# Linear attention into a rational feed-forward layer on one core: the weight conversions go by single chunks, GpSimd's signs move one slot ahead, and the first Newton step stands behind the first pair of chunks

## The chip, the core and the metric

The kernel runs on one core of one Trainium2 chip. The time is what the device takes for one launch, in microseconds (us). Before the change it is 920.56 us, the median of three runs (919.81 to 922.37). One execution was also recorded by the hardware profiler; it took 918.86 us, and its span, from the first to the last instruction, is 917.1 us. Engines are called as in the profile: PE (TensorE's matmuls) with PEld (its weight loads), DVE (VectorE), ACT (ScalarE), POOL (GpSimd), SP (the queue that issues most transfers).

## The reference, cut to what matters

```python
kv  = einsum('bhsd,bhse->bhde', k, v)          # 8 batches, 8 heads, 576 tokens, 64 wide
out = einsum('bhsd,bhde->bhse', q, kv)
rms = sqrt(mean(out * out, axis=-1) + 1e-06)
x   = (out / rms * g_norm)                     # laid out as 4608 tokens x 512
h   = x @ w_in                                 # 512 x 2048
P   = a[0] + a[1]*h + a[2]*h**2 + a[3]*h**3
Q   = 1 + |b[0]|*|h| + |b[1]|*h**2
y   = (P / (Q + 1e-06)) @ w_out                # 2048 x 512
```

`w_in` and `w_out` are float64, all else is float32. The two weight matrices go to the chip as their raw 64-bit words, and the kernel itself makes float32 numbers of them.

## The kernel before, in words

**Tiles and slots.** The 4608 tokens are nine tiles of 512, and the hidden width of 2048 is sixteen chunks of 128. The program walks over 144 *slots* (tile t, chunk c), numbered i = 16 t + c. In a slot, TensorE's first product makes h for the slot that follows (`gemm1`: `h_c`, 128 hidden channels by 512 tokens). ScalarE and VectorE make the rational function of it (`ew_a`, `ew_b`, `ew_c`: d, q and u, the result being g), and TensorE's second product adds the chunk that was finished two slots before to four accumulators (`gemm2`, `acc`). In tile 0 both products take plain float32 operands: a matmul of 128x512 is two instructions, so `h` and `acc` take eight each. From tile 1 on each operand is split into a coarse and a fine part of a faster type, and a product takes three matmuls (lines 445 to 447 and 506 to 508). The attention of tile t+1 runs inside the slots of tile t: `kvp` in slots 1, 3, 5 and 7 of tile 0, `op` in 2, 4, 6 and 8, the mean squares and the Newton step of the norm in slot 9, the norms in 12 and 13, the splitting of x and of the first weights in 14.

**What sets the order.** Each engine takes its instructions in the order in which the program writes them. That order is written out by hand, in slots, and by the table `schedule`, which gives each pair of chunks (a *unit*: `("wi", 4)` is chunks 4 and 5 of `w_in`, `("wo", 2)` chunks 2 and 3 of `w_out`) three slot numbers: when it is fetched, when ScalarE scales it, and when it is split for tile 1. Waits between engines follow from who reads what the other writes.

**Conversion.** A unit lies in memory as `raw`, 128 partitions of 1024 64-bit words, each a low and a high 32-bit word. A chunk is half of it, 512 words. The float32 number is made in four steps: `conv_a` scales the high words (an f32 product, in place) and turns the low words into what has to be added (in place); the sign is brought into the result tile; the high word, shifted left by three bits, is put beside the sign; and the low part is added. For units from `u2` on, `conv_a` is done by ScalarE (line 190, two instructions over 1024 words). The sign is made by GpSimd (`signs`, line 214: high word times 0.0), and VectorE does the other two steps (`conv_c`: line 218, shift and OR; line 222, the addition, a custom instruction). `conv_b` is another form in which VectorE makes the sign itself, with three instructions (lines 208 to 210). The first two units are converted ahead of the slots, with `conv_a` on VectorE (line 188).

**Where conversions stand before.** The list `made` says how many chunks VectorE converts at the end of slot k, in the order in which units are fetched: one in slots 0 and 1, two in 2 and 3, three in 4, two in 5, three in 6, and two in each of 7 to 13. `parts_at` joins two chunks of one unit into one instruction over 1024 words. GpSimd's signs of a chunk are issued in the same slot as its conversion, held back behind that slot's q (line 457), so that they run while VectorE reads h from PSUM. The conversion is the last thing of the slot on VectorE, behind the attention's small subtraction (`kvl`, line 277) and behind the Newton step (lines 287 and 288) in slot 9.

**Ahead of the slots.** VectorE converts chunk 0 with `conv_b` (signs by itself), chunk 1 and chunk 2 with GpSimd's signs, and between chunk 2's two last steps it runs the Newton step of the first tile's norm. Then TensorE spreads the norm over partitions (`rb`, line 620), VectorE multiplies x by it four times (line 621), and chunk 3 is converted. The first product (`h_0`) takes x as it comes.

Of the kernel before, what the change touches and what calls it, by code (L numbers as in the profile page):

```python
# [9 lines left out]
I32 = mybir.dt.int32  # L10
# [13 lines left out]
def linear_attention_then_rational_ffn(  # L24
# [93 lines left out]
    def f32(t):  # L118
        return t.bitcast(F32)
# [27 lines left out]
    def at_slot(step, k):  # L147
        return [u for u in units if schedule[u][step] == k]

    chunks = [(u, j) for u in units for j in range(2)][4:]
    made = {}
    for k, n in enumerate([1, 1, 2, 2, 3, 2, 3] + 7 * [2]):
        made[k], chunks = chunks[:n], chunks[n:]
    assert not chunks

    def unsplit(t, c):
        return t == 0 or t == 1 and c >= LATE
# [31 lines left out]

    def conv_a(u, part=both, engine="S"):
        low, high = words(u, part)
        scale(engine, f32(high), f32(high), 2.0**-112)
        scale(engine, low, low.bitcast(U32), 2.0**-29)

    def room(u):
        kind, c = u
# [3 lines left out]
                w32[kind, c + j] = ups[u][:, j * DM:(j + 1) * DM]  # L202
        return ups[u]

    def conv_b(u, part=both):
        low, high = words(u, part)
        w = room(u).bitcast(I32)[:, part]
        DVE.tensor_scalar(w, high, 3, None, ALU.logical_shift_left)
        DVE.scalar_tensor_tensor(w, high, -(1 << 31), w, ALU.bitwise_and, ALU.bitwise_or)
        DVE.tensor_tensor(w, w, low, ALU.add)  # L210

# [1 line left out]
    def signs(u, part):  # L213
        return POOL.tensor_scalar(room(u)[:, part], f32(words(u, part)[1]), 0.0, None, ALU.mult)

    def conv_c1(u, part):
        w = ups[u].bitcast(I32)[:, part]
        DVE.scalar_tensor_tensor(w, words(u, part)[1], 3, w, ALU.logical_shift_left, ALU.bitwise_or)  # L218

    def conv_c2(u, part):  # L220
        w = ups[u].bitcast(I32)[:, part]
        DVE.tensor_tensor(w, w, words(u, part)[0], ALU.add)

    def conv_c(u, part):
        conv_c1(u, part)
        conv_c2(u, part)

    def parts_at(k):
        out = []
        for u, j in made.get(k, []):  # L230
            if out and out[-1][0] == u:
                out[-1] = u, both
            else:
                out.append((u, (one, two)[j]))
        return out

    def gpart(k, j):
        if k not in gparts:
# [358 lines left out]
        PE.matmul(ms0[p * Q4:(p + 1) * Q4], sel, sq0[p], start=True, stop=True)  # L597
    warm(14, ps_acc.tile([P, TW], F32, tag="acc", name="idle2"))
    u0, u1, u2 = units[:3]
    for u, part in ((u0, two), (u1, one), (u1, two)):  # L600
        signs(u, part)
    conv_a(u0, one, "V")
    conv_b(u0, one)
    conv_a(u0, two, "V")
    conv_c(u0, two)
    conv_a(u1, one, "V")
    conv_c1(u1, one)
    r0 = work.tile([P, TW], F32, tag="u", name="r_0")
    r2 = work.tile([P, TW], F32, tag="u", name="r2_0")
    newton_rstd(ms0, r0, r2)()  # L610
    conv_c2(u1, one)
    ACT.copy(x0[:, NPAIR - 1], o0[NPAIR - 1])
    ACT.activation(b1abs, abg[:, 5:6], AF.Abs)
    conv_a(u2)
    signs(u2, both)
    for p in range(NPAIR):
        pool, tag, bufs = ((ps_h, "h", 2), (ps_h, "h", 2), (ps_at, "at", 1), (ps_at, "ms", 1))[p]
        rb = pool.tile([P, TW], F32, tag=tag, name=f"rb_0_{p}", bufs=bufs)
        ps = slice(p * Q4, (p + 1) * Q4)
        PE.matmul(rb, spread[ps], r0[ps], start=True, stop=True)  # L620
        DVE.scalar_tensor_tensor(x0[:, p], x0[:, p], ghalf, rb, ALU.mult, ALU.mult)
    conv_a(u1, two, "V")
    conv_c(u1, two)


    slots = [(t, c) for t in range(NTILE) for c in range(NF)]
# [1 line left out]
    ph = gemm1(0, 0)  # L628
    for i, (t, c) in enumerate(slots[:-1]):
        q_made = ew_a(t, c, ph)  # L630
        for k, (u, part) in enumerate(parts_at(i) if i > 1 else []):
            made_signs = signs(u, part)
            if k == 0:

                tc.add_manual_dep(made_signs.ins, q_made.ins.name, beside, reason="signs beside h")
        if i:
            ew_d(*slots[i - 1])
        rest = {0: [], 1: [], 2: []}
        ew_b(t, c, ph)
        for u in at_slot(2, i):  # L640
            rest[2].append(split_w(u))
        for u in at_slot(1, i):
            conv_a(u)
        if i >= LAG:
            gemm2(*slots[i - LAG])
            if slots[i - LAG][1] == NF - 1:
                evacuate(slots[i - LAG][0])
        if i < 4:
            ph = gemm1(0, i + 1)
        if t + 1 < NTILE:  # L650
            for step, p in (attention0 if t == 0 else attention)[c]:
# [59 lines left out]
```

## Time and profile before

| what | value |
|---|---|
| median of three runs | 920.56 us |
| profiled execution, its own time | 918.86 us |
| its span | 917.1 us |
| PE busy | 898.5 us (98%) |
| DVE busy | 797.0 us (87%) |
| ACT busy | 685.2 us (75%) |
| POOL busy | 52.7 us (6%), all of it in the first sixth |
| mean granted TensorE clock | 0.996 |

The share of PE is a union of the matmuls' modelled spans, so a PE that is busy may still have been given its work late; the waits and the stretches of the trace tell that. Tile 0, which takes the first sixth of the span, is the only place in which weights are converted, and it is the stretch that the change touches. In a row of the timeline the two first numbers are the start and the time in us, counted from the span's start; what stands in brackets is the idle time of the engine before it and what ended it.

### The profile page before, as it was taken

To read this page: it belongs to the slowest core of one execution; us is meant where nothing else is said; L and a number is where in the kernel's file an instruction comes from. 1 tells how busy PE (TensorE), PEld (TensorE's weight loads), DVE (VectorE), ACT (ScalarE), POOL (GpSimd) and SP (SyncE) were. 2 spreads that over 40 slices of the span, in tenths; PEclk is the share of its full clock that TensorE was granted. 3 is DMA by queue.
4 is the path that set the end of the run, shared out by engine and by line. 5 is a ranking of instruction groups with operands and counts; after the bars stand their busy time and mean duration, and the time that the engine had idled before them with its cause. 6 is when DMAs were issued, how large, how long until landed. Compare 5 with 4: busy or idle time off the path is not lost.

```text
span 917.1 us, 11675 instructions
## 1 busy us (share of the span) xinstructions
PE 898.5 (98%) x4284; PEld 677.8 (74%) x4284; DVE 797.0 (87%) x1237; ACT 685.2 (75%) x1163; POOL 52.7 (6%) x60
## 2 busy tenths in 40 slices
PE   7979998999999999999999999999999999999998
PEld 5434444777768788878887888788887888788886
DVE  3888899999988899889987997889878988898887
ACT  4667776988677768777876787777867787777665
POOL 5134340000000000000000000000000000000000
PEclk9999999999999999999999999999999999999999
DMA  9846100221032012211231213110311020101001
GB/s 368 320 164 232 35 25 30 97 81 47 2 117 72 20 46 89 78 41 48 75 93 41 48 41 117 50 48 21 107 52 48 0 69 13 48 0 46 1 1 46
DMA packets 23961, 65.89 MB, mean 72 GB/s; under 512 B 2336, under 2 KB 2336, under 8 KB 23904
## 3 DMA queue, kind: packets, MB, share of 16 engines
q1 hardware_dynamic: 23328, 64.10, 21.5%
q10 hardware_dynamic: 576, 1.05, 0.3%
q8 instruction: 33, 0.54, 0.2%
q14 instruction: 24, 0.20, 0.1%
HBM read 55.58 MB, written 9.57 MB: 71 GB/s over the span
## 4 chain that ended last, share of the span: by engine, by line
PE 79%; DVE 11%; ACT 6%; issue 2%; DMA 2%; POOL 0%; ACTq 0%; DVEq 0%
PE h L445 12%; PE h L447 12%; PE h L446 12%; PE acc L506 11%; PE acc L507 11%; PE acc L508 11%; PE acc L502 2%; PE kvp L329 2%; DVE q L457 2%; ACT d L466 1%; PE h L441 1%; ACT d L467 1%; DVE u L473 1%; DMA raw_wi<-in_w_in_dram 1%; DVE wow L218 1%
## 5 line engine op out<-in xcount | busy, mean ns | idle before, releaser
L445 PE MATMUL h<-x,parts 128*128 128x512 f32 (+1 forms) x516 | 205.4, 398 | 0.0
L455 ACT ACTIVATE d<-h 128x512 f32<-128x512 f32 x143 | 85.7, 599 | 159.8 <-PE h L447 147.0
L447 PE MATMUL h<-x,parts 128*128 128x512 f32 (+1 forms) x516 | 200.5, 389 | 0.0
L507 PE MATMUL acc<-wol,gh 128*128 128x512 f32 x492 | 191.6, 389 | 0.7 <-DVE wol L259 0.7
L457 DVE SCALAR_TENSOR_TENSOR q<-d,b1abs,q 128x512 f32<-128x512 f32 x143 | 107.1, 749 | 84.5 <-ACT q L456 84.4
L446 PE MATMUL h<-x,wil 128*128 128x512 f32 (+1 forms) x452 | 175.5, 388 | 0.0
L506 PE MATMUL acc<-parts,gl 128*128 128x512 f32 x440 | 171.6, 390 | 0.2 <-DVE gl L490 0.2
L508 PE MATMUL acc<-parts,gh 128*128 128x512 f32 x440 | 171.2, 389 | 0.0
L466 ACT ACTIVATE d<-q,bias 128x512 f32<-128x512 f32 x143 | 105.3, 736 | 36.6 <-DVE q L457 35.7
L445 PEld LDWEIGHTS h<-x,parts 128*128 128x128 f32 x516 | 96.9, 188 | 26.8 <-DVE gl L490 5.0
L447 PEld LDWEIGHTS h<-x,parts 128*128 128x128 f32 x516 | 96.9, 188 | 20.6
L458 ACT ACTIVATE u<-h,na 128x512 f32<-128x512 f32 x143 | 112.0, 783 | 0.0
L473 DVE SCALAR_TENSOR_TENSOR u<-u,na,d 128x512 f32<-128x512 f32 x143 | 107.9, 754 | 0.0
L507 PEld LDWEIGHTS acc<-wol,gh 128*128 128x128 f32 x492 | 92.3, 188 | 20.1 <-DVE wol L259 1.0
L467 ACT ACTIVATE d<-d,bias 128x512 f32<-128x512 f32 x143 | 103.6, 724 | 4.7
L465 DVE SCALAR_TENSOR_TENSOR u<-u,na,h 128x512 f32<-128x512 f32 x143 | 106.2, 743 | 0.7
L471 DVE SCALAR_TENSOR_TENSOR q<-q,d 128x512 f32<-128x512 f32 x143 | 98.5, 689 | 2.9 <-ACT d L467 2.7
L459 DVE TENSOR_TENSOR u<-u,h 128x512 f32<-128x512 f32 x143 | 97.9, 685 | 0.9
L456 ACT ACTIVATE q<-h,abg 128x512 f32<-128x512 f32 x143 | 97.9, 685 | 0.0
L446 PEld LDWEIGHTS h<-x,wil 128*128 128x128 f32 x452 | 85.0, 188 | 16.2 <-issue 0.2
L506 PEld LDWEIGHTS acc<-parts,gl 128*128 128x128 f32 x440 | 82.6, 188 | 18.5 <-DVE gl L490 1.1
L508 PEld LDWEIGHTS acc<-parts,gh 128*128 128x128 f32 x440 | 82.6, 188 | 17.2
(142 smaller groups left out, 1124.4 us busy)
## 6 DMA issues: line engine op xcount, KB each, us to landing
kvm<-in_kv_dram SPq DMA_DIRECT2D x28, 640.0 KB
raw_wo<-in_w_out_dram SPq DMA_DIRECT2D x8, 1024.0 KB
qr<-in_qT_dram SPq DMA_DIRECT2D x32, 256.0 KB
out_dram<-ob SPq DMA_DIRECT2D x16, 512.0 KB
rb<-rd SPq DMA_DIRECT2D x28, 256.0 KB
raw_wi<-in_w_in_dram SPq DMA_DIRECT2D x6, 1024.0 KB
first<-in_first_dram SPq DMA_DIRECT2D x4, 640.0 KB
raw_wi<-in_w_in_dram SPq DMA_DIRECT2D x4, 512.0 KB
```

The costliest lines, as they stand in the source:

```text
L445: PE.matmul(ph, wh, xl, start=(kc == 0), stop=False)
L446: PE.matmul(ph, wl, xh, start=False, stop=False)
L447: PE.matmul(ph, wh, xh, start=False, stop=(kc == NPAIR - 1))
L457: q_made = DVE.scalar_tensor_tensor(q, d, b1abs, q, ALU.mult, ALU.add)
L458: ACT.activation(u, ph, AF.Identity, bias=na[:, 2:3], scale=na[:, 3:4])
L465: DVE.scalar_tensor_tensor(u, u, na[:, 1:2], ph, ALU.add, ALU.mult)
L466: ACT.activation(d, q, AF.Ln, bias=bias[:, 2:3], scale=QSC)
L467: ACT.activation(d, d, AF.Exp, bias=bias[:, 3:4], scale=-1.0)
L473: DVE.scalar_tensor_tensor(u, u, na[:, 0:1], d, ALU.add, ALU.mult)
L506: PE.matmul(o, gl[:, ss], wh, start=(c == 0), stop=False)
L507: PE.matmul(o, gh[:, ss], wl, start=False, stop=False)
L508: PE.matmul(o, gh[:, ss], wh, start=False, stop=(c == NF - 1))
```

## The change

It does five things. (1) Chunks are converted one at a time, in the order in which the products of tile 0 take them: w_out's chunk c, then w_in's chunk c+3, two in each of slots 0 to 13 and the last in slot 15; no two chunks are joined. (2) The first chunk of a slot stands ahead of the attention's work and of the Newton step on VectorE, the second behind. (3) GpSimd's signs are made by whole units, in the slot in which ScalarE scales the unit, which is a slot or more ahead of the conversion. GpSimd therefore reads the high words before ScalarE overwrites them; so ScalarE scales the low words first. (4) Ahead of the slots the signs of chunks 1, 2 and 3 are made by VectorE (`conv_b1` and `conv_b2`, three instructions a chunk), not by GpSimd. (5) The Newton step stands behind the first two chunks; chunk 2's conversion is begun ahead of the four norm products and ended behind them, and chunk 3's is begun before slot 0 and ended in it. PE, ACT and SP keep their order, but for the swap of ScalarE's two scalings.

```diff
-    chunks = [(u, j) for u in units for j in range(2)][4:]
-    made = {}
-    for k, n in enumerate([1, 1, 2, 2, 3, 2, 3] + 7 * [2]):
-        made[k], chunks = chunks[:n], chunks[n:]
-    assert not chunks
+    order = []
+    for c in range(NF):
+        order += [(("wo", c - c % 2), c % 2)]
+        order += [(("wi", c + 3 - (c + 3) % 2), (c + 3) % 2)] if c + 3 < NF else []
+    made = {k: order[2 * k:2 * k + 2] for k in range(NF - 2)}
+    made[NF - 1] = order[2 * (NF - 2):]
...
     def conv_a(u, part=both, engine="S"):
         low, high = words(u, part)
+        scale(engine, low, low.bitcast(U32), 2.0**-29)
         scale(engine, f32(high), f32(high), 2.0**-112)
-        scale(engine, low, low.bitcast(U32), 2.0**-29)
...
-    def conv_b(u, part=both):
+    def conv_b1(u, part):
+        DVE.tensor_scalar(room(u).bitcast(I32)[:, part], words(u, part)[1], 3, None, ALU.logical_shift_left)
+
+    def conv_b2(u, part):
         low, high = words(u, part)
-        w = room(u).bitcast(I32)[:, part]
-        DVE.tensor_scalar(w, high, 3, None, ALU.logical_shift_left)
+        w = ups[u].bitcast(I32)[:, part]
         DVE.scalar_tensor_tensor(w, high, -(1 << 31), w, ALU.bitwise_and, ALU.bitwise_or)
         DVE.tensor_tensor(w, w, low, ALU.add)
...
-    for u, part in ((u0, two), (u1, one), (u1, two)):
-        signs(u, part)
-    conv_a(u0, one, "V")
-    conv_b(u0, one)
-    conv_a(u0, two, "V")
-    conv_c(u0, two)
-    conv_a(u1, one, "V")
-    conv_c1(u1, one)
+    for part in (one, two):
+        conv_a(u0, part, "V")
+        conv_b1(u0, part)
+        conv_b2(u0, part)
     r0 = work.tile([P, TW], F32, tag="u", name="r_0")
     r2 = work.tile([P, TW], F32, tag="u", name="r2_0")
     newton_rstd(ms0, r0, r2)()
-    conv_c2(u1, one)
+    conv_a(u1, one, "V")
+    conv_b1(u1, one)
...
+    signs(u2, both)
     conv_a(u2)
-    signs(u2, both)
     for p in range(NPAIR):
...
         DVE.scalar_tensor_tensor(x0[:, p], x0[:, p], ghalf, rb, ALU.mult, ALU.mult)
+    conv_b2(u1, one)
     conv_a(u1, two, "V")
-    conv_c(u1, two)
+    conv_b1(u1, two)
...
         q_made = ew_a(t, c, ph)
-        for k, (u, part) in enumerate(parts_at(i) if i > 1 else []):
-            made_signs = signs(u, part)
-            if k == 0:
-
-                tc.add_manual_dep(made_signs.ins, q_made.ins.name, beside, reason="signs beside h")
+        for u in at_slot(1, i):
+
+            tc.add_manual_dep(signs(u, both).ins, q_made.ins.name, beside, reason="signs beside h")
...
             conv_a(u)
+        convs = [lambda u=u, j=j: (conv_b2 if u == u1 else conv_c)(u, (one, two)[j]) for u, j in made.get(i, [])]
+        rest[2] += convs[:1]
...
-        for u, part in parts_at(i):
-            rest[2].append(lambda u=u, part=part: conv_c(u, part))
+        rest[2] += convs[1:]
```

VectorE ahead of the slots. `raw_wi_149` is the unit of chunks 0 and 1, `raw_wi_152` that of chunks 2 and 3; `ms` and `r` are the Newton step, `x` the four norm products. Before:

```order
L188 TENSOR_SCALAR raw_wi_149<-raw_wi_149 128x512 x2
L218 SCALAR_TENSOR_TENSOR wiw_280<-raw_wi_149,wiw_280 128x512
L222 ISA wiw_280<-raw_wi_149,wiw_280 128x1024
L188 TENSOR_SCALAR raw_wi_152<-raw_wi_152 128x512 x2
L218 SCALAR_TENSOR_TENSOR wiw_282<-raw_wi_152,wiw_282 128x512
L287 SCALAR_TENSOR_TENSOR r_0_298<-ms_260,r_0_298 128x512
L288 SCALAR_TENSOR_TENSOR r_297<-r_0_298,r_297 128x512
L222 ISA wiw_282<-raw_wi_152,wiw_282 128x1024
L621 SCALAR_TENSOR_TENSOR x_157<-x_157,ghalf,rb_0_311 128x512
```

The same place with the change:

```order
L189 TENSOR_SCALAR raw_wi_149<-raw_wi_149 128x512 x2
L207 TENSOR_SCALAR wiw_282<-raw_wi_149 128x512
L212 SCALAR_TENSOR_TENSOR wiw_282<-raw_wi_149,wiw_282 128x512
L213 ISA wiw_282<-raw_wi_149,wiw_282 128x1024
L275 SCALAR_TENSOR_TENSOR r_0_292<-ms_260,r_0_292 128x512
L276 SCALAR_TENSOR_TENSOR r_291<-r_0_292,r_291 128x512
L189 TENSOR_SCALAR raw_wi_152<-raw_wi_152 128x512 x2
L207 TENSOR_SCALAR wiw_300<-raw_wi_152 128x512
L606 SCALAR_TENSOR_TENSOR x_157<-x_157,ghalf,rb_0_308 128x512
```

Chunk 2's scaling and shift no longer stand ahead of the Newton step but behind it, chunk 2's last two instructions are past the four products of x, and each chunk has one more instruction, the shift.

VectorE in slots 3 and 4, from the end of slot 3's elementwise work to slot 4's conversions. `wow_458` and `wow_370` are w_out's chunks 2 and 3, `wiw_507` and `wiw_417` w_in's 6 and 7, `wow_509` and `wow_466` w_out's 4 and 5. Before:

```order
L479 SCALAR_TENSOR_TENSOR g_3_493<-q_3_451,u_3_452 128x512
L277 TENSOR_TENSOR kvl_136<-kvp_1_474,kvh_130 64x64 x2
L218 SCALAR_TENSOR_TENSOR wow_458<-raw_wo_254,wow_458 128x1024
L222 ISA wow_458<-raw_wo_254,wow_458 128x2048
L457 SCALAR_TENSOR_TENSOR q_4_500<-d_4_499,b1abs,q_4_500 128x512
...
L479 SCALAR_TENSOR_TENSOR g_4_540<-q_4_500,u_4_501 128x512
L218 SCALAR_TENSOR_TENSOR wiw_507<-raw_wi_256,wiw_507 128x1024
L222 ISA wiw_507<-raw_wi_256,wiw_507 128x2048
L218 SCALAR_TENSOR_TENSOR wow_509<-raw_wo_258,wow_509 128x512
L222 ISA wow_509<-raw_wo_258,wow_509 128x1024
```

With the change:

```order
L467 SCALAR_TENSOR_TENSOR g_3_501<-q_3_459,u_3_460 128x512
L222 SCALAR_TENSOR_TENSOR wow_370<-raw_wo_254,wow_370 128x512
L223 ISA wow_370<-raw_wo_254,wow_370 128x1024
L265 TENSOR_TENSOR kvl_136<-kvp_1_482,kvh_130 64x64 x2
L222 SCALAR_TENSOR_TENSOR wiw_417<-raw_wi_256,wiw_417 128x512
L223 ISA wiw_417<-raw_wi_256,wiw_417 128x1024
L445 SCALAR_TENSOR_TENSOR q_4_510<-d_4_509,b1abs,q_4_510 128x512
...
L467 SCALAR_TENSOR_TENSOR g_4_548<-q_4_510,u_4_511 128x512
L222 SCALAR_TENSOR_TENSOR wow_466<-raw_wo_258,wow_466 128x512
L223 ISA wow_466<-raw_wo_258,wow_466 128x1024
L222 SCALAR_TENSOR_TENSOR wiw_417<-raw_wi_256,wiw_417 128x512
L223 ISA wiw_417<-raw_wi_256,wiw_417 128x1024
```

w_out's chunk 2, which `acc` takes first of these, was made with chunk 3 at the end of slot 3; now it is made in slot 2, and slot 3 makes chunk 3 ahead of `kvl` and half of a w_in unit behind it. Slot 4 has two chunks instead of three.

GpSimd, the piece for slots 3 to 6. Before, a unit that is made in two slots has its signs in two instructions:

```order
L214 TENSOR_SCALAR wow_458<-raw_wo_254 128x1024
L214 TENSOR_SCALAR wiw_507<-raw_wi_256 128x1024
L214 TENSOR_SCALAR wow_509<-raw_wo_258 128x512 x2
L214 TENSOR_SCALAR wiw_555<-raw_wi_350 128x512 x2
L214 TENSOR_SCALAR wow_607<-raw_wo_352 128x1024
```

With the change:

```order
L217 TENSOR_SCALAR wow_370<-raw_wo_254 128x1024
L217 TENSOR_SCALAR wiw_417<-raw_wi_256 128x1024
L217 TENSOR_SCALAR wow_466<-raw_wo_258 128x1024
L217 TENSOR_SCALAR wiw_517<-raw_wi_350 128x1024
L217 TENSOR_SCALAR wow_562<-raw_wo_352 128x1024
```

There is one instruction for a unit, and one in each of slots 0 to 12; it is issued one slot ahead of the unit's first conversion, and ScalarE's scaling of the high words stands behind it.

More of the change, by code (lines that the diff above doesn't have):

```diff
@@ L214, in signs, with conv_c @@
         return POOL.tensor_scalar(room(u)[:, part], f32(words(u, part)[1]), 0.0, None, ALU.mult)
-    def conv_c1(u, part):
+    def conv_c(u, part):
+        low, high = words(u, part)
         w = ups[u].bitcast(I32)[:, part]
[L218 to L235, printed above, removed]
+        DVE.scalar_tensor_tensor(w, high, 3, w, ALU.logical_shift_left, ALU.bitwise_or)
+        DVE.tensor_tensor(w, w, low, ALU.add)
     def gpart(k, j):
```

## The prediction

> **What bounds the kernel now.** I read the stretches first, cut where the granted clock changes, then who waits for whom on PE and on DVE. In a row of the stretches the columns are the stretch, its length, then busy time of PE, PEld, DVE, ACT and POOL, the granted clock, the share of the DMA engines and GB/s; in a row of waits the total, the number and the longest, in us.
>
> ```profile
> 24.88:28.29 3.41, 3.41 (x4) 1.48 (x5) 3.38 (x7) 0.00 (x0) 0.44 (x1) 0.50 1.04 413
> 28.29:59.01 30.72, 25.84 (x98) 11.49 (x97) 25.44 (x38) 25.27 (x41) 5.71 (x2) 1.00 0.73 267
> 59.01:62.42 3.41, 3.41 (x5) 1.35 (x6) 3.29 (x5) 2.85 (x4) 2.84 (x2) 0.50 0.00 0
> 62.42:145.70 83.28, 83.28 (x241) 37.05 (x239) 74.10 (x97) 58.05 (x88) 29.99 (x13) 1.00 0.26 89
> 148.80:166.80 18.00, 17.34 (x78) 11.12 (x78) 17.05 (x26) 13.77 (x23) 0.00 (x0) 1.00 0.17 51
> 166.80:900.00 733.20, 732.92 (x3631) 591.21 (x3632) 647.93 (x1022) 561.62 (x962) 0.00 (x0) 1.00 0.17 51
> PE acc L502 <- DVE wow L222: 3.8, 1, 3.8
> PE h L446 <- DVE parts L259: 2.6, 1, 2.6
> PE rb L620 <- DVE r L288: 2.4, 1, 2.4
> PE h L441 <- DVE wiw L222: 1.1, 1, 1.1
> PE h L441 <- DVE x L621: 0.9, 1, 0.9
> PE acc L507 <- DVE wol L259: 0.7, 1, 0.7
> DVE q L457 <- ACT q L456: 5.3, 2, 2.7
> DVE kvl L277 <- ACT kvf L272: 2.0, 3, 1.0
> DVE r L287 <- ACT r L284: 1.9, 1, 1.9
> ```
>
> From 166.8 on PE has no hole (732.92 of 733.20): whatever is gained ahead of that carries to the end one for one, whatever is gained behind it is nothing. Ahead of it PE waits only for DVE. Two of these waits (2.4 for the Newton step, 3.8 for w_out's chunk 2) are each followed by 3.41 us at half clock, which costs 1.7 us more. From 62.4 to 145.7 PE is full, and DVE is nearly so (74.10 of 83.28). The last two waits that PE has, at the change of tiles (parts) and at 166 (wol), are DVE's lateness. So the forecast is: **how much earlier does DVE end tile 0?**
>
> **Ahead of the slots.** Timeline of DVE, POOL, ACT and PE:
>
> ```profile
> 13.44 0.77 DVE L188 TENSOR_SCALAR raw_wi<-raw_wi 128x512 f32<-128x512 f32 x2 [13.44 <-DMA raw_wi<-in_w_in_dram]
> 14.76 1.89 POOL L214 TENSOR_SCALAR wiw<-raw_wi 128x512 f32<-128x512 f32 x1 [7.94 <-DMA raw_wi<-in_w_in_dram]
> 15.30 1.01 DVE L210 CUSTOM_DVE_ANT_0 wiw<-raw_wi,wiw 128x1024 uint16<-128x1024 uint16 x1
> 16.68 0.76 DVE L188 TENSOR_SCALAR raw_wi<-raw_wi 128x512 f32<-128x512 f32 x2 [0.37 <-POOL wiw L214]
> 18.71 0.63 ACT L284 ACTIVATE r<-r 128x512 f32<-128x512 f32 x1
> 19.47 1.21 DVE L188 TENSOR_SCALAR raw_wi<-raw_wi 128x512 f32<-128x512 f32 x2 [0.37 <-POOL wiw L214]
> 21.20 0.68 DVE L287 SCALAR_TENSOR_TENSOR r<-ms,r 128x512 f32<-128x512 f32 x1
> 21.20 2.15 ACT L190 ACTIVATE raw_wo<-raw_wo 128x1024 f32<-128x1024 f32 x2 [1.28 <-DMA raw_wo<-in_w_out_dram]
> 22.41 2.90 POOL L214 TENSOR_SCALAR wow<-raw_wo 128x1024 f32<-128x1024 f32 x1 [1.27 <-ACT raw_wo L190]
> 22.52 1.61 DVE L222 CUSTOM_DVE_ANT_0 wiw<-raw_wi,wiw 128x1024 uint16<-128x1024 uint16 x1
> 24.05 2.71 DVE L621 SCALAR_TENSOR_TENSOR x<-x,ghalf,rb 128x512 f32<-128x512 f32 x4
> 28.07 0.69 DVE L222 CUSTOM_DVE_ANT_0 wiw<-raw_wi,wiw 128x1024 uint16<-128x1024 uint16 x1
> 30.27 0.60 ACT L455 ACTIVATE d<-h 128x512 f32<-128x512 f32 x1 [6.93 <-PE h L441]
> 31.48 0.75 DVE L457 SCALAR_TENSOR_TENSOR q<-d,b1abs,q 128x512 f32<-128x512 f32 x1 [2.72 <-ACT q L456]
> 50.65 3.70 PE L441 MATMUL h<-x,wiw 128*128 128x512 f32 x8 [1.07 <-DVE wiw L222]
> ```
>
> Now, GpSimd's signs pace DVE there: two waits of 0.37, and the custom addition takes 1.01 beside POOL against 0.69 alone. With the change no signs run before w_out's first unit lands (21.2, by ACT's row). Chunk 0 then ends near 15.9; chunk 1 takes 0.7 (scaling), 0.4 (shift) and 1.4, and ends near 18.5. ScalarE's square ends at 19.34, so the Newton step starts at 19.4 instead of 21.20 and ends at 20.8. Chunk 2's scaling and shift (three instructions of some 0.4) go to 21.9, and there the signs of w_out's first unit set in beside them. That collision the trace shows at 19.47 (1.21 for two, against 0.76) and at 22.52 (1.61 against 0.69): 0.45 to 0.92. I take 0.45, since the shift is of the kind of the first row. So x starts at 22.3 instead of 24.05. The first of the four products takes some 0.7, so `h_0` starts at 23.1.
>
> Then the clock. Before, PE waited 2.4 and 0.9 us shortly ahead of the half clock at 24.88; with the Newton step 1.8 earlier it is 0.6 and 0.9. Waits of 1.1 and 2.6 elsewhere brought no half clock (the stretches after 28.29 and 148.80 show 1.00), so I take full clock: `h_0` takes the 3.70 of the last row and ScalarE's d starts at 26.85 instead of 30.27. DVE's first q comes at 28.05 instead of 31.48. DVE is free by then: x to 24.95, chunk 2's last two 1.33, chunk 3's three 1.13, so 27.4. **Gain 3.4 us**; with the half clock all the same, 2.1; with a collision of 0.92 as well, about 1.2.
>
> **In the slots.** Rows of DVE, POOL and ACT, and two groups of DVE over the first 110 us:
>
> ```profile
> 43.83 0.74 DVE L457 SCALAR_TENSOR_TENSOR q<-d,b1abs,q 128x512 f32<-128x512 f32 x1
> 48.12 1.22 DVE L218 SCALAR_TENSOR_TENSOR wiw<-raw_wi,wiw 128x1024 int32<-128x1024 int32 x1
> 50.52 0.74 DVE L457 SCALAR_TENSOR_TENSOR q<-d,b1abs,q 128x512 f32<-128x512 f32 x1
> 69.94 0.75 DVE L457 SCALAR_TENSOR_TENSOR q<-d,b1abs,q 128x512 f32<-128x512 f32 x1 [2.62 <-ACT q L456]
> 75.36 0.69 DVE L218 SCALAR_TENSOR_TENSOR wow<-raw_wo,wow 128x512 int32<-128x512 int32 x1
> 78.03 0.74 DVE L457 SCALAR_TENSOR_TENSOR q<-d,b1abs,q 128x512 f32<-128x512 f32 x1
> 44.66 2.86 POOL L214 TENSOR_SCALAR wiw<-raw_wi 128x1024 f32<-128x1024 f32 x1 [19.35 <-DVE q L457]
> 80.36 3.34 POOL L214 TENSOR_SCALAR wow<-raw_wo 128x1024 f32<-128x1024 f32 x1
> 45.99 2.22 ACT L190 ACTIVATE raw_wi<-raw_wi 128x1024 f32<-128x1024 f32 x2
> L473 DVE SCALAR_TENSOR_TENSOR u<-u,na,d 128x512 f32<-128x512 f32 x10 | 8.7, 870 | 0.0
> ```
>
> *Narrow chunks cost.* A joined unit takes 48.12 to 50.52, 2.40; two chunks apart 75.36 to 78.03, 2.67. Eleven units are joined before, none after: 11 x 0.27 = +3.0. Chunk 3's two last instructions come into the slots: +1.3. Together **+4.3**.
>
> *Waits go.* The 2.6 at 69.94 is the echo of PE's 3.8: PE stood for w_out's chunk 2, so `h_5` came late. Now chunk 2 is made in slot 2. PE's walk from 23.1 at 3.44 for each `h` and `acc` (3.70 less the overlap with the next) has it asked for at 49.9, and DVE ends it at 28.05 + 6.95 + 7.45 + 4.29 + 1.33 = 48.1 (slots of 4.29 elementwise, 2.67 conversion, 0.5 `kvl` in odd ones). The tightest is the very first `acc`: asked at 34.3, made at 33.7. `kvl`'s 2.0 goes too, since a chunk of 1.33 now stands ahead of it. The Newton step of slot 9 waits 1.9; ahead of it comes a chunk (-1.33), but ScalarE is 0.55 later there (next), so 0.7 goes. **-5.3**.
>
> *Collisions go.* Where GpSimd had two instructions in a slot, the second ran into DVE's: L473 takes 0.870 in the mean of ten against 0.75 undisturbed, 1.2 us in two of them, and a g (L479) loses 0.4. One instruction a slot, behind q, is the case of 44.66, with no such loss. **-1.6**.
>
> *What the new wait costs.* ScalarE's high half now waits for the signs: they run from 0.83 to 3.69 behind q, and the high half would start at 3.2. So ScalarE is 0.55 later, and what is queued behind it is the attention's evacuation and the next slot's d and q. In slots 2, 4, 6 and 8 that makes the next q possible at 6.95 to 7.0 behind the last, where DVE's own work takes 6.95: a tie, **+0.2** in all. In odd slots DVE needs 7.45 and covers it; in 0, 10 and 11 ScalarE has less to do.
>
> Sum in the slots: 4.3 - 5.3 - 1.6 + 0.2 = -2.4. Bounds: no wait but the 2.6 goes and ScalarE's delay shows in five slots, +0.6; everything as the rows' starts read, slot by slot, -3.6. I take -2.7, inside it and nearer the second, as the starts include small gaps that the durations leave out.
>
> **Beyond tile 0.** PE's work from `h_0` to tile 1's first product is 30 x 3.44 and about 8 for the attention, so it is there at 134.3. DVE's parts, which let PE go on at 148.80 before, come 7.4 earlier (the 6.1 below and the 1.3 of slot 15's chunk, which stands behind them), at 141.4. PE's 2.6 therefore *grows* to some 6.5, and if half clock follows as in 59.01:62.42, 1.7 is lost behind it. PE then comes to wol's place 5.7 earlier at worst, and DVE ends wol 6.1 earlier where PE had waited 0.7: DVE still ends that wait. So the end moves by DVE's gain: 3.4 + 2.7 = **6.1 us**. The profiled execution goes from 918.86 to 912.8; it stands 1.7 below the median, so 920.56 - 6.1 = 914.5.
>
> Where only a page has a price: the Trainium skill, SBUF — State Buffer, "Who interferes with whom", says that a VectorE instruction in a two-port mode or with two SBUF inputs and a GpSimd instruction lock each other out of a shared port, and the loser "fully blocks". By it the shift at 21.5 would wait for the whole 2.9 of the signs, and the start would gain nothing. The trace shows 0.45 and 0.92, not 2.9; so I hold to the rows and keep it as the first rival.
>
> **Rivals.**
>
> 1. *The signs of w_out's first unit hold DVE ahead of x.* They start at 21.2, run 2.9 to 24.1, and x would start at 24.5. For: every DVE instruction that met a start of POOL there was stretched. Against: never by over 0.92. The start's gain is then 0 and only the slots' 2.7 is left: 917.9. Chance 0.1.
>
> 2. *ScalarE becomes the bound, and the kernel slower.* Place: the high half behind the signs. If the signs take x longer than 2.86, five slots (2, 4, 6, 8, 9) lose x, four (1, 3, 5, 7) lose x - 0.7, three (0, 10, 11) x - 1. Break-even with 6.1 is at x = 1.0, signs of 3.9. Should DVE's two-input q and u (0.69 and 0.75 a slot) hold them, x is 1.4: 7.0 + 2.8 + 1.2 = 11 us, and the time is 920.56 - 6.1 + 11 = 925.5. For: 3.34 at 80.36. Against: that one stood behind another; those that start at q's end take 2.86 with both in them. Chance 0.07.
>
> 3. *The conversion isn't early enough.* The first `acc` has 0.6 us to spare. If it or the third stalls PE as before, the 2.6 stays, a half clock with it: the slots give 0, the start 3.4, time 917.1. Chance 0.1.
>
> Forecast 0.65; what is not listed 0.08, spread around it. The forecast's own range is 913.1 (7.4 gained: no collision at the start, 3.8, and 3.6 in the slots) to 917 (half clock at the start, 2.1, and 1.5 in the slots, midway between their bounds). **Chances.** 0.3% is 2.8 us, about what a measurement of this kernel can tell from no change. Faster: 0.64 from the forecast, 0.05 of rival 1, 0.07 of rival 3, 0.05 of the rest, 0.81. Slower: 0.07 of rival 2 and 0.01. Same: 0.11. Range 911.8 to 918.4.
>
> **What would show it.** Newton's L287 (now 275) at 19.4 and x at 22.3; full clock at 24.9; DVE's first q near 28; no wait of PE for wow; the wait for parts at the change of tiles grown to about 6.5, with half clock behind it; signs of 2.86, and ScalarE waiting some 0.5 for them in each of the slots 0 to 12. It is wrong if ScalarE's q ends DVE's waits in slot after slot, if x starts behind 24, or if PE gets a new wait behind 166.8.

## The result and the profile after

The changed kernel takes 912.92 us, the median of four runs (912.59 to 914.15), beside 920.18 for the kernel before: the ratio is 0.9921, with an interval from 0.9899 to 0.9943. The forecast was 914.5, its range 911.8 to 918.4. The profiled execution took 912.63 us (predicted 912.8). The medians are 7.3 us apart and the two profiled executions 6.2: beside the experiments the kernel before ran at mean granted clocks from 0.990 to 0.996 (spans from 921.5 down to 916.8 us), the changed kernel ran at 0.996 to 1.000, and the profiled execution of the kernel before is one of those with 0.996.

The page of the changed kernel, its span and the line of busy times:

```profile
span 910.8 us, 11692 instructions
...
PE 897.3 (99%) x4284; PEld 678.2 (74%) x4284; DVE 798.0 (88%) x1262; ACT 687.7 (76%) x1163; POOL 45.8 (5%) x55
```

DVE has 1 us more to do than before and the kernel is still 6.3 us shorter: what went is waiting. Who waits for whom on PE (total, number, longest):

```profile
PE h L434 <- DVE parts L247: 2.6, 1, 2.6
PE op L343 <- DVE kvl L265: 1.6, 1, 1.6
PE h L429 <- DVE x L606: 1.4, 1, 1.4
PE acc L495 <- DVE wol L247: 0.6, 1, 0.6
PE rb L605 <- DVE r L276: 0.5, 1, 0.5
```

The waits for converted weights (3.8 and 1.1) are gone, that for the Newton step fell from 2.4 to 0.5. One wait is new: `op` for `kvl`. The stretches, with the columns that the prediction names:

```profile
56.03:137.20 81.17, 81.17 (x235) 36.40 (x236) 75.66 (x116) 62.13 (x92) 25.84 (x9) 1.00 0.27 91
137.20:141.15 3.95, 1.11 (x4) 0.22 (x2) 3.84 (x6) 3.37 (x7) 0.00 (x0) 1.00 0.00 0
142.63:146.05 3.42, 3.42 (x8) 2.28 (x7) 3.19 (x6) 2.54 (x5) 0.00 (x0) 0.50 0.00 0
160.50:893.70 733.20, 732.97 (x3631) 591.20 (x3632) 648.12 (x1021) 562.44 (x962) 0.00 (x0) 1.00 0.17 51
```

Two stretches of half clock in tile 0 (behind 24.88 and 59.01) are gone, one has come behind the change of tiles. Behind 160.5 nothing changed. DVE's q marks the slots, so its starts in the timeline say where the 6.3 us come from ("the last q" below is that of slot 142; slot 143 is done in two halves):

| q of slot | before, us | after, us | moved | what lies between |
|---|---|---|---|---|
| 0 | 31.48 | 28.57 | -2.91 | the start |
| 4 | 58.76 | 57.34 | -1.42 | chunk 3's end and narrow chunks, against `kvl`'s waits |
| 5 | 69.94 | 64.36 | -5.58 | PE's wait for w_out's chunk 2 (2.6), slot 4's third chunk (1.1) and a collision, gone |
| 7 | 86.97 | 78.89 | -8.08 | collisions with GpSimd (1.4) and slot 6's third chunk (1.1), gone |
| 14 | 141.22 | 133.56 | -7.66 | narrow chunks, Newton |
| 16 | 154.06 | 147.74 | -6.32 | the last chunk, in slot 15 |
| 142, the last whole one | 900.13 | 893.82 | -6.31 | nothing |

### The profile page after: what moved, and what is told of

Read it like the earlier page. It is cut to its first block, busy times and chain, and to the rows that moved or that the text cites. A ratio compares the mean times of both kernels' runs of the same rounds, so it can differ in the third digit from the quotient of the medians.

```text
span 910.8 us, 11692 instructions
## 1 busy us (share of the span) xinstructions
PE 897.3 (99%) x4284; PEld 678.2 (74%) x4284; DVE 798.0 (88%) x1262; ACT 687.7 (76%) x1163; POOL 45.8 (5%) x55
## 4 chain that ended last, share of the span: by engine, by line
PE 78%; DVE 6%; issue 6%; ACT 3%; POOL 3%; DMA 2%; ACTq 0%; SPq 0%; POOLq 0%; DVEq 0%
PE h L433 13%; PE h L435 12%; PE h L434 12%; PE acc L494 12%; PE acc L495 12%; PE acc L496 12%; POOL wow L217 2%; PE kvp L317 2%; POOL wiw L217 2%; PE acc L490 2%; DMA raw_wo<-in_w_out_dram 1%; DMA first<-in_first_dram 1%; DVE q L445 1%; ACT d L454 1%; PE ms L361 1%
```

## The experiments

All are edits of the changed kernel. The ratio, with its 95% interval, is to runs of the kernel before that were made beside them on the same chip (medians of 920.0 to 921.33).

| run | edit | median, us (runs) | ratio |
|---|---|---|---|
| e1_start_old | the start as before | 916.85 (8) | 0.9951 [0.9935, 0.9968] |
| e2_slots_old | the slots as before | 920.11 (10) | 0.9990 [0.9976, 1.0005] |
| e3_behind | both conversions behind `kvl` and Newton | 919.19 (10) | 0.9979 [0.9967, 0.9991] |
| e4_signs_same | signs by chunks, in the conversion's slot | 916.70 (6) | 0.9954 [0.9936, 0.9972] |
| e5_gate | w_out's first signs held back | 912.07 (4) | 0.9915 [0.9900, 0.9930] |
| e7_pe_extra | 2.6 us of unused matmuls in slot 12 | 912.74 (4) | 0.9926 [0.9907, 0.9945] |
| e8_pool_split | two subtractions for tile 1 on GpSimd | 913.90 (4) | 0.9937 [0.9920, 0.9954] |
| e9_joined | chunks joined again from slot 7 on | 911.09 (4) | 0.9906 [0.9887, 0.9925] |
| e10_joined_gate | e9 and e5 | 909.27 (4) | 0.9871 [0.9855, 0.9887] |
| e11_joined5_gate | joined from slot 5 on, and e5 | **908.87** (4) | 0.9864 [0.9849, 0.9879] |
| e12_start_old_fill | e1 with e7's matmuls | 916.87 (4) | 0.9949 [0.9933, 0.9965] |

**The two halves apart.** e1 brings back the start: GpSimd's signs for chunks 1 to 3, Newton behind chunk 2's shift, chunk 3 ended ahead of the slots. e2 (second diff) brings back the list `made` with its joined chunks at the slot's end and the signs in the same slot.

```diff
-    for part in (one, two):
-        conv_a(u0, part, "V")
-        conv_b1(u0, part)
-        conv_b2(u0, part)
+    for u, part in ((u0, two), (u1, one), (u1, two)):
+        signs(u, part)
...
+    conv_c(u0, two)
+    conv_a(u1, one, "V")
+    conv_c1(u1, one)
...
     newton_rstd(ms0, r0, r2)()
-    conv_a(u1, one, "V")
-    conv_b1(u1, one)
+    conv_c2(u1, one)
...
     made[NF - 1] = order[2 * (NF - 2):]
+    made[0] = made[0][:1]
```

> The part ahead of the slots is as before the change (GpSimd's signs for chunks 1 to 3, the Newton step behind chunk 2's shift), the slots are as changed; slot 0 has only w_out's chunk 0, since chunk 3 is done ahead of it. Theory A (VectorE's end of tile 0 sets the time): first q back at 31.5, second q 1.6 us later than in the changed kernel (one chunk of 1.3 less in slot 0), the rest in step, so the time is 912.9 + 1.6 = 914.5. Theory B (TensorE's own holes and half clock set it): the wait for the Newton step and its 3.4 us of half clock come back, 1.9 + 1.7, so 916.5.

```diff
-    made = {k: order[2 * k:2 * k + 2] for k in range(NF - 2)}
+    for k, n in enumerate([1, 1, 2, 2, 3, 2, 3] + 7 * [2]):
+        made[k], chunks = chunks[:n], chunks[n:]
...
-        for u in at_slot(1, i):
+        for k, (u, part) in enumerate(parts_at(i) if i > 1 else []):
...
-        rest[2] += convs[1:]
+        for u, part in parts_at(i):
+            rest[2].append(lambda u=u, part=part: conv_c(u, part))
```

> The part ahead of the slots is as changed, the slots are as before (old list of chunks, joined units, signs in the slot of the conversion, conversions last); chunk 3 is ended in slot 0. Theory A: second q 1.6 us earlier than before the change, TensorE's wait for w_out's chunk 2 is still there, each slot as long as before, so 920.2 - 1.6 = 918.6. Theory B: TensorE comes earlier to a wait that VectorE ends at its own time, so most of the start's gain is lost there, 920.

By the ratios the new slots alone gain 0.49%, the new start alone 0.10% with an interval that takes in none, and both together 0.79%. The intervals are too wide to say that 0.49 and 0.10 don't add up to 0.79; e2's trace shows that the start's gain is lost there, and how. Its start is as early as the changed kernel's; timeline of PE with one stretch, and timeline of DVE:

```profile
48.88 5.40 PE L437 MATMUL h<-x,wiw 128*128 128x512 f32 x8 [2.40 <-DVE wiw L231]
...
58.77 1.60 PE L498 MATMUL acc<-wow,g 128*128 128x512 f32 x2 [3.75 <-DVE wow L231]
```

```profile
49.05:52.46 3.41, 3.41 (x5) 1.35 (x6) 3.18 (x6) 2.96 (x5) 2.85 (x1) 0.50 0.74 232
```

```profile
28.39 0.75 DVE L453 SCALAR_TENSOR_TENSOR q<-d,b1abs,q 128x512 f32<-128x512 f32 x1 [0.56 <-ACT q L452]
...
48.75 0.74 DVE L453 SCALAR_TENSOR_TENSOR q<-d,b1abs,q 128x512 f32<-128x512 f32 x1
...
55.74 0.46 DVE L273 TENSOR_TENSOR kvl<-kvp,kvh 64x64 fp32r<-64x64 f32 x2 [2.62 <-ACT kvf L268]
...
58.63 0.74 DVE L453 SCALAR_TENSOR_TENSOR q<-d,b1abs,q 128x512 f32<-128x512 f32 x1
```

The same subtraction in the kernel before:

```profile
55.86 0.46 DVE L277 TENSOR_TENSOR kvl<-kvp,kvh 64x64 fp32r<-64x64 f32 x2 [0.98 <-ACT kvf L272]
```

The first q is 3.1 us ahead of the kernel before. Of that 1.3 is chunk 3's end, which slot 0 now has to do; the q of slot 3 is 1.8 ahead (48.75 and 50.52), and that of slot 4 only 0.13. What takes the 1.8 is the half clock. PE, started earlier, stands for the unconverted chunk of w_in for 2.4 instead of 1.1, a stretch of half clock follows that the kernel before doesn't have there, and `h` takes 5.40 instead of 3.70. `kvp`, behind it on PE, comes late, so DVE waits 2.62 instead of 0.98 ahead of `kvl`, makes w_out's chunk 2 hardly earlier than before, and PE stands for it until 58.8 as before. An engine that starts earlier only to wait longer can lose its gain to the clock. (At the change of tiles e2's profiled execution loses 2.2 more with two stretches of half clock, of which more below.)

With the new slots both waits are gone, and the same start is worth 3.9 by the medians (916.85 to 912.92) and 0.30%, or 2.8, by the ratios. Of that, part is the clock: e1's start falls into two stretches of half clock, so that its first q comes at 33.00, 1.5 later than in the kernel before. e1 takes back the order of the Newton step and VectorE's signs for chunks 1 to 3 together; no run separates the two.

**Is it the place of the chunks?** e3 puts both chunks of a slot behind the attention's work, the rest as changed.

```diff
-        rest[2] += convs[:1]
...
-        rest[2] += convs[1:]
+        rest[2] += convs
```

> As changed, but both conversions of a slot stand behind the attention's subtraction and behind the Newton step. Theory A: VectorE waits for ScalarE again, some 1.2 us in each of slots 1, 3, 5 and 7 and 1.3 more in slot 9, all of it carried to the end: 912.9 + 6 = 919. Theory B: TensorE has 3 to 4 us of waiting at the change of tiles and is full ahead of it, so VectorE's delay shows only beyond that: 913 to 915.

Slots 1, 3, 5 and 7 are each 1.1 to 1.2 us longer (8.6 instead of 7.43 to 7.51) and slot 9 is 1.3 longer; q of slot 14 starts at 139.29, 5.7 later, and of the gain of 0.79% only 0.21% is left. DVE in slot 1 and PE in slot 3 of this kernel:

```profile
40.88 0.46 DVE L265 TENSOR_TENSOR kvl<-kvp,kvh 64x64 fp32r<-64x64 f32 x2 [1.07 <-ACT kvf L260]
```

```profile
56.92 2.29 PE L343 MATMUL op<-qr,kvf 128*128 128x64 f32 x4 [2.46 <-DVE kvl L265]
```

DVE waits 1.07 for ScalarE ahead of `kvl`, and this wait is what the first chunk fills in the changed kernel. Narrow chunks that don't fill it give three quarters of the gain back.

**Is it the signs?** e4 issues the signs chunk by chunk in the slot of the conversion.

```diff
-        for u in at_slot(1, i):
-            tc.add_manual_dep(signs(u, both).ins, q_made.ins.name, beside, reason="signs beside h")
+        for k, (u, j) in enumerate([x for x in made.get(i, []) if x[0] not in (u1, u2)]):
+            made_signs = signs(u, (one, two)[j])
+            if k == 0: tc.add_manual_dep(made_signs.ins, q_made.ins.name, beside, reason="signs beside h")
```

> As changed, but GpSimd's signs are made chunk by chunk in the slot of the conversion, two instructions a slot, the first held behind q. Theory A, with collisions: the second instruction of each slot meets an instruction of VectorE with two inputs in SBUF and stretches it by 0.4 to 0.9, in some 12 slots, and ScalarE no longer waits for signs: 5 to 10 us more on VectorE, 918 to 922. Rival: the stretched rows of before were due to something else in those slots; then nothing is lost and the time is 913 or a little less.

The time is 916.70, 3.8 over the changed kernel and a little under what was expected. Slots 2 to 13 are 0.38 to 0.40 longer each, but for slot 9, which is 0.5 shorter. POOL and DVE in slot 4 of e4:

```profile
58.81 1.54 POOL L217 TENSOR_SCALAR wow<-raw_wo 128x512 f32<-128x512 f32 x1 [4.29 <-DVE q L445]
60.33 2.04 POOL L217 TENSOR_SCALAR wiw<-raw_wi 128x512 f32<-128x512 f32 x1
```

```profile
60.88 1.15 DVE L461 SCALAR_TENSOR_TENSOR u<-u,na,d 128x512 f32<-128x512 f32 x1
```

The second GpSimd instruction of a slot takes 2.04 where the first takes 1.54, and the u beside it 1.15 where it takes 0.75 alone. One instruction a slot, right behind q, takes 2.86 to 2.89 in every slot of the changed kernel and stretches nothing. PE has no wait for w_out's chunk 2 in e4: that went by the order of the chunks, not by the signs.

**The collision at the start.** e5 holds w_out's first signs back until chunk 2's shift.

```diff
+    held = mybir.DependencyInfo(mybir.DependencyClass.Sync, mybir.DependencyReason.DATA)
-    signs(u2, both)
+    tc.add_manual_dep(signs(u2, both).ins, shifted.ins.name, held, reason="signs behind the shift")
```

> As changed, but GpSimd's signs of w_out's first unit are held until chunk 2's shift on VectorE is done, ahead of the four products of x. Theory A: the scaling of chunk 2 takes 0.76 instead of 1.69, x starts at 21.9, the first q at 27.7, and the whole is 0.9 us earlier: 912.0. ScalarE's high half then ends near 26.0, just ahead of its first d. Theory B (start matters only through TensorE's holes): TensorE's wait for x shrinks by 0.9, the same time. Rival: the signs, now beside x's products, stretch those instead, and nothing is gained: 912.9.

The changed kernel, timeline of DVE and of POOL:

```profile
19.42 0.69 DVE L275 SCALAR_TENSOR_TENSOR r<-ms,r 128x512 f32<-128x512 f32 x1 [0.67 <-ACT r L272]
...
20.75 1.69 DVE L189 TENSOR_SCALAR raw_wi<-raw_wi 128x512 int32<-128x512 uint32 x2
...
22.82 2.72 DVE L606 SCALAR_TENSOR_TENSOR x<-x,ghalf,rb 128x512 f32<-128x512 f32 x4
...
28.57 0.75 DVE L445 SCALAR_TENSOR_TENSOR q<-d,b1abs,q 128x512 f32<-128x512 f32 x1 [0.56 <-ACT q L444]
```

```profile
21.01 2.88 POOL L217 TENSOR_SCALAR wow<-raw_wo 128x1024 f32<-128x1024 f32 x1 [14.19 <-DMA raw_wo<-in_w_out_dram]
```

and with the signs held back:

```profile
20.71 0.76 DVE L189 TENSOR_SCALAR raw_wi<-raw_wi 128x512 int32<-128x512 uint32 x2
...
22.16 2.72 DVE L607 SCALAR_TENSOR_TENSOR x<-x,ghalf,rb 128x512 f32<-128x512 f32 x4 [0.23 <-PE rb L606]
...
27.91 0.75 DVE L445 SCALAR_TENSOR_TENSOR q<-d,b1abs,q 128x512 f32<-128x512 f32 x1 [0.56 <-ACT q L444]
```

The two scalings take 1.69 beside the start of the signs and 0.76 without: the collision costs 0.93. Of it 0.66 arrives at the first q and 0.62 at the last (893.20), since x then has to wait 0.23 for `rb`. The medians, 912.07 against 912.92, agree with that, though the intervals of the two ratios overlap: it is the traces that show it.

**Does PE's wait at the change of tiles count?** e7 puts three matmuls, whose product nobody reads, into slot 12. It gives PE 2.6 us more to do ahead of that wait.

```diff
+        if i == 12:
+            extra = ps_at.tile([P, TW], F32, tag="ms", name="extra", bufs=1)
+            for _ in range(3): PE.matmul(extra, w32["wi", 12][:, 0:P], x0[:, 0], start=True, stop=True)
```

> As changed, with three extra matmuls of 128x512 in float32 (2.6 us of TensorE) in slot 12 behind the next slot's first product; their result is not used. Theory A: they fall into the 3.1 us for which TensorE waits at the change of tiles, and the time is the same within 0.5: 912.9. Theory B: TensorE is full there and pays all: 915.5.

Who waits on PE in e7, and two of its stretches:

```profile
PE h L434 <- DVE parts L247: 0.6, 1, 0.6
```

```profile
158.18:161.59 3.41, 1.62 (x6) 1.12 (x7) 3.27 (x4) 3.41 (x8) 0.00 (x0) 1.00 0.29 106
161.59:165.00 3.41, 3.41 (x16) 2.28 (x16) 2.42 (x5) 3.38 (x7) 0.00 (x0) 0.50 0.55 204
```

The wait shrank from 2.6 to 0.6, q of slot 16 starts at 147.68 (147.74), and the time is the same. PE had slack there; DVE's end of tile 0 is the bound. The half clock moved to 161.59; the last q is 0.12 later by it at most.

**More off DVE's end.** If DVE's end of tile 0 sets the time, each us taken from DVE there must reach the end. e9 joins the two chunks of a unit again from slot 7 on, where no chunk is wanted soon; e10 adds e5's edit, e11 joins from slot 5 on. e8 takes another way: GpSimd makes two subtractions of the splitting, one in slot 14 and one in slot 16.

```diff
-    made = {k: order[2 * k:2 * k + 2] for k in range(NF - 2)}
-    made[NF - 1] = order[2 * (NF - 2):]
+    made = {k: order[2 * k:2 * k + 2] for k in range(7)}
+    pair = lambda *u: [(u, 0), (u, 1)]
+    made[7] = [(("wo", 6), 1)] + pair("wi", 10)
+    for k, u in enumerate((("wo", 8), ("wi", 12), ("wo", 10), ("wi", 14), ("wo", 12), ("wo", 14))):
+        made[8 + k] = pair(*u)
```

In e11 the first list has five slots, slot 5 makes w_out's chunk 5 and w_in's 8 and 9, and the whole units begin in slot 6. e8, on the changed kernel:

```diff
-            DVE.tensor_tensor(wl, w, f32(wh), ALU.subtract)
+            (POOL if u in units[:2] else DVE).tensor_tensor(wl, w, f32(wh), ALU.subtract)
```

> As changed up to slot 6; from slot 7 on units are joined again (one chunk and a unit in slot 7, a unit in each of slots 8 to 13, none in 15). Theory A: seven joined units save 7 x 0.27 = 1.9 us of VectorE ahead of wol, and at the change of tiles it is 0.6 earlier (1.3 of slot 15's chunk comes ahead of it); TensorE has 0.96 of waiting to give at wol, so the end is 1.5 us earlier: 911.4. Theory B: nothing, 912.9. Rival: a unit made whole comes too late for one of the products, and the time is 914 or more.

> As changed, but the fine parts of w_in's first two units are subtracted by GpSimd instead of VectorE (slots 14 and 16). Theory A: 2.3 us less on VectorE ahead of wol; but the first of them is what TensorE waits for at the change of tiles, and on GpSimd it ends some 1.5 later than on VectorE if it takes 3 us like the signs; so wol is 2.3 earlier and the change of tiles 0.5 to 1.5 later than now: 912 to 914. If GpSimd's subtraction also stretches VectorE's splits of x beside it, up to 916.

> The joined units from slot 7 on together with GpSimd's signs held behind chunk 2's shift. VectorE's end of tile 0 as the one limit: 2.66 and 0.65 us (the shifts of the 17th q in the two runs that had one each) add up, so 912.9 - 3.3 = 909.6. If TensorE is the limit by now, its remaining wait at the change of tiles (2.6) still leaves room, so no loss is expected; less than 2.9 in all would say that something else ends first.

> The same, with units joined from slot 5 on (a chunk and a unit in slot 5, a unit in each of slots 6 to 13). VectorE's end: two more joined units at 0.27, 909.6 - 0.5 = 909.1. Rival: w_out's chunk 6 or w_in's chunks 10 and 11 then come too late for TensorE, which stands at the old distance from VectorE there; 910 or more.

DVE in slots 9 and 16 of e9:

```profile
101.36 0.69 DVE L287 SCALAR_TENSOR_TENSOR r<-ms,r 128x512 f32<-128x512 f32 x1
...
145.07 0.74 DVE L457 SCALAR_TENSOR_TENSOR q<-d,b1abs,q 128x512 f32<-128x512 f32 x1
```

The Newton step in slot 9 has no wait left, because a whole unit stands ahead of it (1.1 before; that slot is 1.27 shorter). Slots 10 to 13 are 0.26 shorter each, slot 15 is 1.33 shorter and slot 7 is 1.07 longer: 2.67 in all at slot 16, and 2.66 at the last q (891.16). Between the q of slot 16 and the last q lie 746.07 to 746.09 us in the kernel before, the changed one, e5, e9, e10 and e11 alike. By the medians e9 gains 1.8, its runs lying between 909.89 (the profiled one) and 912.86. e10 adds up (the last q at 890.52, 3.30 earlier; 2.66 and 0.62). e11 gets a little more: 908.87, 4 us below the changed kernel and the fastest of all.

e8 went the wrong way: q of slot 16 is 0.75 later than in the changed kernel, the last q 1.2. POOL and DVE, and who waits on PE:

```profile
136.97 2.36 POOL L247 TENSOR_TENSOR parts<-wiw,parts 128x1024 fp32r<-128x1024 f32 x1 [16.19 <-ACT parts L240]
```

```profile
137.45 2.43 DVE L288 TENSOR_TENSOR x<-xf,x 128x512 fp32r<-128x512 f32 x1 [0.76 <-ACT x L284]
...
153.04 1.87 DVE L332 TENSOR_TENSOR ql<-qr,qh 128x512 fp32r<-128x512 f32 x1
```

```profile
PE h L433 <- DVE x L288: 2.5, 3, 2.0
```

The wait for parts turned into one for the split x, and slot 14 is 0.6 longer on DVE (9.18). GpSimd's subtraction takes 2.36 where DVE's takes 1.22, but what lengthens the slot is DVE's split of x beside it: 2.43 instead of 0.69, 1.74 more, against the 1.14 that DVE is spared. In slot 16 `ql` beside the second one takes 1.87 instead of 0.69, and that slot gains nothing either.

**The half clock at the change of tiles.** e1 has 6.8 us of it there, the changed kernel 3.4. e12 is e1 with e7's matmuls, which fill the hole ahead of it.

> The old part ahead of the slots with the new slots, and three unused matmuls (2.6 us of TensorE) in slot 12. In the run without them TensorE stood still at the change of tiles and had two stretches of 3.4 us at half clock behind it, and slots 16 and 17 were 0.45 and 0.27 longer than in the changed kernel. If the half clock is what lengthened them, the extra work keeps the clock up and the time falls by 0.7, to 916.1; if not, it stays at 916.85, or rises by up to 2.6 if TensorE has no room.

The trace answers, the time doesn't. In e12 there is no half clock at that place, and the slots 16 and 17 take 6.89 and 8.17 as in the changed kernel, against 7.35 and 8.44 in e1: two stretches cost 0.7, one costs nothing. But e12's first q came 0.56 later than e1's, and the medians are equal.

## Why the prediction held, point by point

**What bounds.** Right: DVE's end of tile 0 is the time. e5, e9 and e10 carry their gain there to the end within 0.04 us in their traces, and e7's extra work on PE costs nothing. That the sum of 6.1 came so near to the 6.3 of the traces is in part luck: the start was put 0.5 too high and the slots 0.7 too low. The time came out 1.6 under 914.5 because the medians moved by 7.3.

**The start: predicted 3.4, measured 2.9.** Chunks 0 and 1 and the Newton step came as worked out (L275 at 19.42, predicted 19.4), and the clock was full from 24.88 on. The step that was off is the collision: 0.45 was taken, the lower of its two rows, "since the shift is of the kind of the first row". It was 0.93, the upper bound; and the signs hit the scalings, not the shift. So x started at 22.82, not 22.3, and the first q at 28.57, not 28.05. The first rival (signs holding DVE for the whole 2.9) is out. Of the 2.9, x gives 1.2 (`h_0` starts at 23.62 instead of 24.84), and the half clock that is gone 1.7 (the first d comes 3.74 behind that start instead of 5.43), so more than half of it hung on the clock. The full clock was argued from the length of PE's waits, which by the last section doesn't decide it: that it came is partly luck, with 1.93 us of work in the window 19.75:23.16 where the bound is near 1.5 or 1.6.

**The slots: predicted 2.7, measured 3.4.** The stretch from the first q to that of slot 16, before and after:

```profile
31.48:154.06 122.58, 115.10 (x353) 52.01 (x352) 110.48 (x149) 90.67 (x139) 38.54 (x15) 0.99 0.33 117
```

```profile
28.57:147.74 119.17, 114.75 (x352) 52.32 (x351) 112.12 (x174) 92.13 (x139) 37.32 (x13) 0.99 0.36 130
```

DVE is busy 1.6 longer and idle 5.05 less. I also took every instruction of DVE in these slots from its start to the next one's start, idle time of over 0.25 counted as a wait:

| term | predicted | measured |
|---|---|---|
| conversions (narrow chunks, chunk 3's end) | +4.3 | +4.17 (34.43 to 38.60) |
| waits gone (2.62, 1.99, 0.82) | -5.3 | -5.43 |
| collisions | -1.6 | -2.15, all else of the elementwise work in it |
| ScalarE behind the signs | +0.2 | in the term above |

The last two terms together were predicted at -1.4 and are -2.15; the other two were right to 0.15. The prediction's own sum was -2.4, of which it made -2.7. Two groups of DVE show most of it, before and after:

```profile
L473 DVE SCALAR_TENSOR_TENSOR u<-u,na,d 128x512 f32<-128x512 f32 x16 | 13.2, 824 | 0.0
...
L479 DVE SCALAR_TENSOR_TENSOR g<-q,u 128x512 f32<-128x512 f32 x16 | 11.5, 717 | 1.1
```

```profile
L461 DVE SCALAR_TENSOR_TENSOR u<-u,na,d 128x512 f32<-128x512 f32 x16 | 11.9, 746 | 0.0
...
L467 DVE SCALAR_TENSOR_TENSOR g<-q,u 128x512 f32<-128x512 f32 x16 | 11.1, 692 | 1.1
```

Durations give 1.7; the rest lies between the instructions, which a stretched one also pushes apart. "Everything as the rows' starts read, slot by slot" gave -3.6 and was the better of the two countings.

ScalarE's waits for the signs, and DVE's for ScalarE, over the same slots:

```profile
ACT raw_wo L191 <- POOL wow L217: 2.8, 7, 0.4
ACT raw_wi L191 <- POOL wiw L217: 2.4, 6, 0.4
```

```profile
DVE r L275 <- ACT r L272: 1.1, 1, 1.1
...
DVE q L445 <- ACT q L444: 0.6, 1, 0.6
```

ScalarE waits in each of the slots 0 to 12, 0.4 instead of 0.55, and no q waits for it but the first: the tie went DVE's way, and the second rival (ScalarE as the bound) is out. PE has no wait for converted weights, so the third is out too.

**The change of tiles: right in its effect, wrong in its size.** PE's wait for parts was to grow from 2.6 to 6.5; it stayed at 2.6, 3.1 with the gap around it. PE was to arrive at 134.3 and was free at 137.8, 3.5 later: 0.5 is its later start, 1.6 its standing for `kvl` (until 56.03), and the rest, some 1.4, is work that the count of "30 x 3.44 and about 8" had too low. That wait the prediction didn't name: `kvp` and `op` take turns in one PSUM buffer, `kvl` is what reads `kvp` last, and `kvl` now stands behind a chunk. It cost nothing, since PE had the time. The half clock behind the wait came, and was as free as the wait (slots 16 and 17 take 6.89 and 8.18, as in the kernel before).

## What to carry to other kernels

Ask of every gain which wait comes next, and whether the clock drops behind it: the early start was worth 0.1% by itself, no more than noise, and some 3 to 4 us, part of it the clock, once the next waits were gone, so the two halves must be tried together as well as apart. Fill an engine's wait with the work that is needed soonest, and keep work that isn't needed soon in its cheapest form: narrow chunks paid where TensorE stood for one of them or a wait could be filled (slots 0 to 4), and cost 0.27 us a pair elsewhere. Where the rows give two sizes of a collision and nothing separates them, hold back the starting instruction rather than guess: one dependency was worth 0.6 us. Work that goes to GpSimd isn't off VectorE while the two collide: e8 spared VectorE 1.14 and cost it 1.74.

## What the runs showed of the hardware

**A GpSimd start costs VectorE 0.3 to 1.7 us, by what VectorE begins next.** On DVE 1.69 instead of 0.76 at the start; 1.15 instead of 0.75 in e4, where POOL pays too (2.04 instead of 1.54); 2.43 instead of 0.69 in e8. Beside the signs, all but two of the stretched instructions in the thirteen traces are the first that VectorE begins behind a start of GpSimd, up to 0.7 us behind it, and none of them has an operand in PSUM (the two others are scalings at the starts of e1 and e12, 0.70 instead of 0.42). Where the first one reads h, or `rb` in e5, from PSUM, it keeps its time (0.75), and instructions on SBUF alone that come later beside the signs in the slots keep theirs (0.69 and 0.75). The Trainium skill, SBUF — State Buffer, "Who interferes with whom", has the shared port as an exclusive lock on which the loser blocks. Beside the signs, which have one operand, the measured stretch is a third of the 2.88 us that they take at the start, and a fifth of the 2.04 in e4, so there the loser isn't held for a whole instruction. Beside e8's subtractions, which have two, it is: VectorE's `x` and `ql` end 0.55 behind the end of GpSimd's, as if they had begun only then.

**The half clock goes by fixed windows of 3.41 us.** In each trace its stretches, but for the one at the trace's end, are 3.41 or 6.83 long, and they start whole windows apart (142.63 and 910.63 in the changed kernel: 225.0 times 3.413). Windows on that grid near the change of tiles, of the kernel before, the changed one, e1 and e4 in turn; the third column is PE's busy time, the granted clock is behind POOL's:

```profile
144.34:147.75 3.41, 1.87 (x5) 0.57 (x3) 2.79 (x5) 3.41 (x8) 0.00 (x0) 1.00 0.00 0
147.75:151.16 3.41, 2.36 (x10) 1.99 (x11) 3.37 (x6) 1.08 (x2) 0.00 (x0) 1.00 0.00 0
```

```profile
139.22:142.63 3.41, 1.48 (x7) 1.25 (x8) 3.41 (x6) 1.35 (x3) 0.00 (x0) 1.00 0.00 0
```

```profile
140.43:143.84 3.41, 1.37 (x4) 0.23 (x2) 2.99 (x5) 3.41 (x7) 0.00 (x0) 1.00 0.00 0
143.84:147.26 3.42, 2.57 (x6) 2.12 (x7) 3.38 (x6) 1.05 (x3) 0.00 (x0) 0.50 0.00 0
147.26:150.67 3.41, 3.41 (x8) 2.31 (x8) 3.18 (x5) 1.57 (x3) 0.00 (x0) 0.50 0.00 0
```

```profile
136.95:140.37 3.42, 1.50 (x4) 0.38 (x2) 3.07 (x5) 2.32 (x4) 0.00 (x0) 1.00 0.00 0
140.37:143.78 3.41, 0.49 (x1) 0.19 (x1) 2.80 (x5) 3.41 (x8) 0.00 (x0) 1.00 0.00 0
```

Behind the changed kernel's window stands 142.63:146.05, shown above, at 0.50. A window at full clock with 1.77 or more of work is followed by full clock (the lowest is in e4, 55.03:58.44); one with 1.48 or less is followed by half. Between lie only e4's 1.50 (full) and e7's 1.62 (half, above), so the bound is near 1.5 or 1.6. A second stretch follows where the first was busy for 2.0 to 2.8 of its 3.41 us (e1's 2.57), and none where it was busy 3.2 or more: at half clock that is work of 1.0 to 1.4 and of 1.6 at full clock, so one bound fits both. It fits all the windows of the thirteen traces between 14 and 165 us but that one pair; no run was made to test it. It means that the same wait of 2.6 us is free of half clock or not by where the grid cuts it, as in the kernel before and the changed one, and that a forecast can't know it from the length of the wait. The Trainium skill, TensorE: Matmul & The Clock Gate, "Part 1: The HAM clock gate", gives a free-running window of 3413 ns, which the distances agree with; its idle window as the condition is too strict here, where 1.48 us of work in a window weren't enough.
